# Two blocks of a seven-product dense layer by turns, with finer weight jobs and another order of operands, in a fused FNet, Mish and gate kernel

## The chip, the cores and the metric

The kernel runs on one core of a Trainium2 chip. The metric is the device time of one execution in microseconds (us); lower is better. Times are from executions on the chip; one further execution was recorded by the hardware profiler.

## What is computed

The input x is 2048 x 640, in float32. Two branches are mixed by a gate:

```
g = sigmoid((x * gate_w).sum(-1))                 # one value per row
a = C_re @ (x @ Wd_re.T) - C_im @ (x @ Wd_im.T)   # 2048 x 2048 and 640 x 640 DFT matrices
h = x @ w1 + b1;  b = mish(h) @ w2                # 640 -> 1728 -> 640, mish(v) = v * tanh(softplus(v))
out = g * a + (1 - g) * b
```

The change lies in the first dense product, x @ w1, with its bias and Mish.

## The kernel before

**Arithmetic.** TensorE (PE) multiplies blocks of 128 x 128 by 128 x 512. For float32 accuracy each operand is split in a high and a low part (`split`, L82: a copy on ScalarE, ACT, L80, and a subtraction on VectorE, DVE, L77), and one product takes three matmuls (`mm3`, L91). The large products are done in the Strassen-Winograd way: seven products of half-size blocks in place of eight, at the price of sums of the operands beforehand and sums of the results behind.

**Order of work.** The whole program is a list of steps, each with matmuls for PE, the preparation of its operands (splits, sums, and the loads that these need), and work behind it (`post`, `at`). The loop at L967 writes the instructions out in that order: at step i it first runs the preparations of all steps up to i + 7 (i + 6 in the dense stage, `LEAD_D`), issuing loads of up to nine steps further ahead (`AHEAD`) while more than three buffers are free; then the matmuls of step i, stores that are due, the work behind the step, and then, as long as its own clock says that DVE is more than 1 us behind PE and `wait_until` allows it, parts of jobs that have no fixed place (L1006). Each engine runs its instructions in the order in which they were written out, and each waits for its own operands. All loads and stores go through SP's queue (loads L978, stores L987), in order too.

**Jobs.** A job is a generator that stops at each `yield`. `job_go` (L151) sets `wait_until = i + yielded value`: with 0 the next part may follow in the same step, with 1 in the next step at the earliest. `w1_job` (L552) splits the weights of one block and makes their sums, in four parts. Behind the w1 jobs follow y products (`gate_y`), and then the weights of the output stage ("top", w2c, w2r and "low" jobs). `need` runs a job's remaining parts at once where a step's preparation wants them. No job parts are started in steps from four before to twelve after the start of the dense stage (`quiet`).

**Buffers.** There are 20 of 128 x 512 in float32 (f), 10 pairs for split operands (rh, rl; some more are lent from the weights' buffers), 26 pairs for split weights (wh, wl), 4 for raw weights (fx), and 8 PSUM banks (ps). Each kind is a list from which the longest free one is taken. A buffer that was stored can be taken again as soon as its store has been written out; the load or copy into it waits until the store has landed. A result is stored three steps after it was made. A job that loads f buffers is only taken up if its own and eight more are free.

**The dense stage** has 104 steps, counted here from 0. Steps 0 to 7 compute the columns of h that the blocks leave over (`dense_rest`). The other columns are six blocks fp = 0 to 5, each of the column chunks fa = fp and fb = fp + 6. `dense_first` does them for the first half of the rows (tp = 0, steps 8 to 55), and then for the second half (tp = 1, steps 56 to 103); the output stage follows at 104. A block takes one turn of eight steps:

| step of the turn | operand | bank | matmuls | work behind it |
|---|---|---|---|---|
| 0 p1 | a11 | a (new) | 6 | ACT copies a into an f buffer ("snap") |
| 1 p5 | s1 | b (new) | 6 | snap of b |
| 2 | d2 | d (new) | 3 | none |
| 3 p6 | s2 | a goes on | 6 | snap of a, called u2 |
| 4 p3 | s4, d1 | b goes on | 9 | DVE adds u2 to b; Mish; b is free |
| 5 p7 | s3 | a goes on | 6 | DVE adds a to the snap of b |
| 6 p2 | a12, d1 | c (new) | 9 | DVE adds c and d to the snaps; c, d free; Mish one and two steps later |
| 7 p4 | a22, d2 | a goes on | 9 | Mish of a two steps later, then a is free |

The operands (x and its sums s1 to s4) are split once for each half and kept in rh/rl buffers through its six turns; `free` gives them back in the turn of the last block. `sums_of` (L687) loads four blocks of x and makes the four sums, for k = 0 and 1. At which step each is prepared is written out by hand in the lists at L939 and L941; a preparation listed for step n runs six steps earlier.

Of the kernel before, what the change touches and what calls it, by code (L numbers as in the profile page):

```python
# [10 lines left out]
OP = mybir.AluOpType  # L11

S, D, F = 2048, 640, 1728
P = 128
# [7 lines left out]
FP = 6  # L22
# [23 lines left out]
def fnet_mish_gate(ctx: ExitStack, tc: tile.TileContext, xn, xt, c_re, c_im, wd_re, wd_im,  # L46
# [28 lines left out]
    def tt(o, a, b, op):  # L75
        clock["dve"] += 0.14 + 0.54 * a.shape[-1] / N
        nc.vector.tensor_tensor(o, a, b, op=op)  # L77

    def copy(o, a, scale=1.0):
        nc.scalar.activation(o, a, AF.Copy, scale=scale)  # L80
# [10 lines left out]
    def mm3(ps, ah, al, bh, bl, start, stop):  # L91
        mm(ps, ah, bh, start, False)
        mm(ps, ah, bl, False, False)
        mm(ps, al, bh, False, stop)

    def part(w, a, b):
        return w[0][:, a:b], w[1][:, a:b]
# [454 lines left out]
    def w1_job(f, ga, gb):  # L552
        t = FS.get()
        a, b, c = W.get(), W.get(), W.get()
        if f % KD == 0:
            T2B[f // KD] = W.get()
        split(*a, ga)
        split(*part(b, 2 * P, 5 * P), gb[:, 2 * P:])
        yield 0

        tt(ga[:, A2], gb[:, A2], ga[:, A2], OP.subtract)
        tt(gb[:, A2], gb[:, B2], gb[:, A2], OP.subtract)
        tt(t[:, A2], gb[:, B2], ga[:, A2], OP.subtract)
        tt(t[:, B2], ga[:, B2], t[:, A2], OP.subtract)
        yield 0
        split(*part(b, 0, 2 * P), t[:, B2])
        split(*part(c, 0, 2 * P), ga[:, A2])
        yield 0
        split(*part(c, 2 * P, 4 * P), gb[:, A2])
        split(*part(c, 4 * P, 5 * P), t[:, :P])  # L570
        split(*part(T2B[f // KD], f % KD * P, f % KD * P + P), t[:, P:2 * P])
        FS.put(t)
        FX.put(ga, gb)
        W1[f] = (a, b, c)
# [106 lines left out]
    def dense_first(tp, end, ops):  # L681


        t1, t2 = 2 * tp, 2 * tp + 1
        n0 = len(steps)

        def sums_of(k):  # L687
            raw = [(("xs", tp, a, k), xt[t, kk])
                   for a, t, kk in ((21, t2, k), (22, t2, k + 2), (11, t1, k), (12, t1, k + 2))]

            def prep():
                a21, a22, a11, a12 = (RAW.pop(r[0]) for r in raw)
                s1 = FS.get()
                tt(s1, a21, a22, OP.add)
                tt(a21, a11, a21, OP.subtract)
                tt(a22, s1, a11, OP.subtract)
                tt(a12, a12, a22, OP.subtract)
                FS.put(a11)
                XS[k] = {"s1": s1, "s2": a22, "s3": a21, "s4": a12}
            return raw, prep  # L700

        def make(name):
            def prep():
                if name[0] == "s":
                    for k in range(2):
                        x_split((name, k, tp), XS[k].pop(name))
                elif name[0] == "d":
                    x_split((name, 0, tp), RAW.pop(("xd", tp, name)))
                else:
                    for k in range(2):  # L710
                        x_split((name, k, tp), RAW.pop(("xo", tp, name, k)))
            return prep

        def sub(fp, ops, then=()):

            def mms():
                a, b, c = W1[fp]
                for bank, name, blk, start, stop in ops:
                    if start:
                        H[bank] = psum.get()  # L720
                    for k in range(2):
                        mm3(H[bank], *blk(a, b, c, k), *X[name, k, tp], start and k == 0, stop and k == 1)
                for bank, name, w, start, stop in then:
                    if start:
                        H[bank] = psum.get()
                    mm3(H[bank], *part((a, b)[w], 4 * P, 5 * P), *X[name, 0, tp], start, stop)
            return mms

        def at_cols(which, c0):
            return lambda a, b, c, k: part((a, b, c)[which], c0 + k * P, c0 + k * P + P)  # L730

        def t2_at(fp):
            return lambda a, b, c, k: part(c, 4 * P, 5 * P) if k == 0 else \
                part(T2B[fp // KD], fp % KD * P, fp % KD * P + P)

        def snap(name, bank):
            f = KEEP[name] = FS.get()
            copy(f, H[bank])

        def pop(bank):  # L740
            psum.put(H.pop(bank))

        def add(bank, f):
            tt(f, H[bank], f, OP.add)
            return f

        def out_act(f, t, o, src):
            mish(o, src, f)
            store(asc[f][t], o, o)

        for fp in range(FP):
            fa, fb = fp, fp + FP
            over = fp == FP - 1

            def free(*names, over=over):
                if over:
                    x_free(*[(n, k, tp) for n in names for k in range(2 if n[0] != "d" else 1)])

            def p1_post(free=free):
                snap("p1", "a")  # L760
                free("a11")

            def p5_post(free=free):
                snap("p5", "b")
                free("s1")

            def p6_post(free=free):
                snap("u2", "a")
                free("s2")

            def p3_post(free=free, fb=fb):
                o = add("b", KEEP.pop("u2"))
                pop("b")
                out_act(fb, t1, o, o)
                free("s4")

            def p7_post(free=free):
                add("a", KEEP["p5"])
                free("s3")

            def p2_post(free=free, fa=fa, fb=fb):
                c11, c22 = add("c", KEEP.pop("p1")), add("d", KEEP.pop("p5"))
                pop("c")
                pop("d")
                i = clock["step"]
                at(i + 1, lambda: out_act(fa, t1, c11, c11))
                at(i + 2, lambda: out_act(fb, t2, c22, c22))
                free("a12", "d1")

            def p4_post(free=free, fa=fa, fp=fp):  # L790
                ps = H.pop("a")

                def last():
                    out_act(fa, t2, FS.get(), ps)
                    psum.put(ps)
                at(clock["step"] + 2, last)
                free("a22", "d2")
                if end:
                    W.put(*W1[fp])
                    if fp in (KD - 1, FP - 1):  # L800
                        W.put(T2B[fp // KD])

            step([], [lambda fp=fp: need(("w1", fp))], sub(fp, [("a", "a11", at_cols(0, 0), True, True)]), p1_post)
            step([], [], sub(fp, [("b", "s1", at_cols(2, 0), True, True)]), p5_post)
            step([], [], sub(fp, [], [("d", "d2", 1, True, True)]))
            step([], [], sub(fp, [("a", "s2", t2_at(fp), False, True)]), p6_post)
            step([], [], sub(fp, [("b", "s4", at_cols(1, 2 * P), False, False)], [("b", "d1", 1, False, True)]), p3_post)
            step([], [], sub(fp, [("a", "s3", at_cols(2, 2 * P), False, True)]), p7_post)
            step([], [], sub(fp, [("c", "a12", at_cols(0, 2 * P), True, False)], [("c", "d1", 0, False, True)]), p2_post)
            step([], [], sub(fp, [("a", "a22", at_cols(1, 0), False, False)], [("a", "d2", 0, False, True)]), p4_post)  # L810
        for name, i in ops:
            if name[0] == "k":
                raw, prep = sums_of(int(name[1:]))
                steps[i][0].extend(raw)
                attach.append((i, prep))
                continue
            kk = {"a11": (t1, 0), "a12": (t1, 2), "a22": (t2, 2), "d1": (t1, 4), "d2": (t2, 4)}.get(name)
            if name[0] == "d":
                steps[i][0].append((("xd", tp, name), xt[kk]))
            elif kk:  # L820
                steps[i][0].extend((("xo", tp, name, k), xt[kk[0], kk[1] + k]) for k in range(2))
            attach.append((i, make(name)))
# [107 lines left out]
    for tp in range(2):  # L930
# [7 lines left out]
    n0 = nd + 8  # L938
    dense_first(0, False, [("k0", n0 + 2), ("k1", n0 + 2), ("s1", n0 + 3), ("s2", n0 + 4), ("s4", n0 + 6), ("s3", n0 + 7)])  # L939
    n0 = len(steps)  # L940
    dense_first(1, True, [("a11", n0 - 1), ("k0", n0), ("k1", n0 + 1), ("s1", n0 + 1), ("d2", n0 + 2), ("s2", n0 + 3),  # L941
                          ("s4", n0 + 4), ("d1", n0 + 4), ("s3", n0 + 5), ("a12", n0 + 6), ("a22", n0 + 7)])
    narrow.update(range(nd, len(steps)))
    quiet = range(nd - 4, nd + 13)
    n_dense = len(steps)
# [114 lines left out]
```

## Time and profile before

| | |
|---|---|
| median of 3 runs | 891.66 us (891.64 to 891.80) |
| the profiled execution, its time | 893.29 us |
| its span | 891.4 us |
| PE's mean granted clock | 0.996 of full |
| moved to and from memory | 215.22 MB, mean 241 GB/s |

The profile names instructions by engine, line and tiles (f<-ps is a write of an f buffer from a PSUM bank). Since splits, sums and copies go through helpers, their line is the helper's: L77 is any DVE operation on two tensors, L80 any ACT copy, L89 any matmul, L618 Mish. The view of waits lists for each engine what it waited for, with the sum, the number of times and the longest. In the timeline a row is start, duration, engine, line, operation and tiles, and in square brackets the idle time before it and what ended it. Matmuls overlap: each is recorded with 0.39 us, and the next starts some 0.23 us after it. A table by stretches gives the busy time of each engine in windows counted from the start of the span.

### The profile page before, as it was taken

The page shows a single profiled execution, that of the slowest core. Times are in us where ns is not written, and L with a number is a line of the kernel's source. Part 1 is how long each engine was busy: PE and PEld are TensorE (multiplying, and loading weights), DVE is VectorE, ACT ScalarE, POOL GpSimd, SP SyncE. Part 2 cuts the span into 40 slices and gives each one's busy share as a digit, 9 for nine tenths or more (in the row PEclk, how much of TensorE's full clock was granted, in tenths as well). Part 3 has the DMA queues.
Part 4 walks back from the last instruction along what each step waited for, and adds up shares of the span by engine and source line. Part 5 has one row for each costly group of instructions (what it writes and reads, how often), then busy time and mean ns, then how long its engine had stood idle before and what let it go on. Part 6 is the DMA issues. An engine that isn't in the chain of part 4 may idle for free.

```text
span 891.4 us, 12188 instructions
## 1 busy us (share of the span) xinstructions
PE 864.6 (97%) x3780; PEld 711.3 (80%) x3780; DVE 714.5 (80%) x1243; ACT 479.3 (54%) x910; POOL 0.2 (0%) x4
## 2 busy tenths in 40 slices
PE   8999999999999999999999999898899999999995
PEld 6888888888888888888888888687688788888884
DVE  5899997899799668998997987764844897689986
ACT  5665645454565545647665576544555665442630
POOL 0000000000000000000000000000000000000000
PEclk9999999999999999999999999999999999999998
DMA  9865669597979564768868793589575667467753
GB/s 321 309 214 186 238 209 308 154 318 235 319 268 335 207 217 160 262 226 268 282 213 290 263 316 135 181 309 358 194 260 176 240 226 246 144 229 238 268 208 129
DMA packets 118064, 215.22 MB, mean 241 GB/s; under 512 B 13424, under 2 KB 15600, under 8 KB 118000
## 3 DMA queue, kind: packets, MB, share of 16 engines
q1 hardware_dynamic: 118000, 214.46, 70.3%
q8 instruction: 29, 0.48, 0.2%
q14 instruction: 35, 0.29, 0.1%
HBM read 168.80 MB, written 45.61 MB: 241 GB/s over the span
## 4 chain that ended last, share of the span: by engine, by line
PE 91%; DVE 4%; DMA 2%; issue 1%; ACT 1%; SPq 0%; DVEq 0%; ACTq 0%
PE ps L89 91%; DVE f L77 2%; DMA act<-f 1%; DVE wl L77 1%; DVE fx L77 1%; DMA f<-in_xn_dram 1%; ACT wh L80 0%; DVE rl L77 0%; SPq L978 0%; ACT rh L80 0%; ACT f L618 0%; ACT f L80 0%; DMA f<-in_xt_dram 0%; SPq L958 0%; SPq L987 0%
## 5 line engine op out<-in xcount | busy, mean ns | idle before, releaser
L89 PE MATMUL ps<-rh,wh 128*128 128x512 f32 x1067 | 416.6, 391 | 8.1 <-ACT f L80 3.9
L89 PE MATMUL ps<-rh,wl 128*128 128x512 f32 x1053 | 410.2, 390 | 0.0
L89 PE MATMUL ps<-rl,wh 128*128 128x512 f32 x1052 | 409.8, 390 | 0.0
L80 ACT ACTIVATE rh<-f 128x512 fp32r<-128x512 f32 x412 | 243.6, 624 | 150.8 <-DVE f L77 104.1
L77 DVE TENSOR_TENSOR rl<-f,rh 128x512 fp32r<-128x512 f32 x410 | 266.7, 685 | 51.3 <-ACT rh L80 50.7
L89 PEld LDWEIGHTS ps<-rh,wh 128*128 128x128 f32 x1067 | 200.8, 188 | 52.7 <-ACT f L80 5.6
L89 PEld LDWEIGHTS ps<-rh,wl 128*128 128x128 f32 x1053 | 198.2, 188 | 41.1
L89 PEld LDWEIGHTS ps<-rl,wh 128*128 128x128 f32 x1052 | 198.2, 188 | 41.2
L77 DVE TENSOR_TENSOR f<-f,f 128x512 f32<-128x512 f32 x311 | 212.9, 689 | 15.0 <-DMA u<-f 5.4
L80 ACT ACTIVATE f<-ps 128x512 f32<-128x512 f32 (+1 forms) x147 | 86.5, 595 | 104.5 <-PE ps L89 82.8
L77 DVE TENSOR_TENSOR f<-ps,f 128x512 f32<-128x512 f32 x87 | 57.4, 686 | 56.5 <-PE ps L89 56.5
L80 ACT ACTIVATE wh<-f 128x512 fp32r<-128x512 f32 (+2 forms) x160 | 70.1, 477 | 50.7 <-DVE f L77 41.3
L77 DVE TENSOR_TENSOR wl<-f,wh 128x512 fp32r<-128x512 f32 (+2 forms) x159 | 75.5, 505 | 19.2 <-ACT wh L80 19.0
L89 PE MATMUL ps<-wh,wh 128*128 128x512 f32 x201 | 78.8, 392 | 6.5 <-DVE f L77 4.2
L89 PE MATMUL ps<-wl,wh 128*128 128x512 f32 x196 | 76.3, 389 | 0.0
L89 PE MATMUL ps<-wh,wl 128*128 128x512 f32 x195 | 75.9, 389 | 0.0
L77 DVE TENSOR_TENSOR wl<-fx,wh 128x640 fp32r<-128x640 f32 (+3 forms) x80 | 42.3, 551 | 16.9 <-ACT wh L80 16.9
L618 ACT ACTIVATE f<-f,b1s 128x512 f32<-128x512 f32 x36 | 25.9, 720 | 51.9 <-DVE f L77 51.9
L89 PEld LDWEIGHTS ps<-wh,wh 128*128 128x128 f32 x201 | 37.7, 188 | 16.5 <-DVE f L77 5.0
L80 ACT ACTIVATE wh<-fx 128x128 fp32r<-128x128 f32 (+5 forms) x81 | 39.2, 511 | 6.8 <-DMA fx<-in_xn_dram 2.7
L89 PEld LDWEIGHTS ps<-wl,wh 128*128 128x128 f32 x196 | 36.8, 188 | 7.4
L89 PEld LDWEIGHTS ps<-wh,wl 128*128 128x128 f32 x195 | 36.6, 188 | 7.6
(40 smaller groups left out, 162.4 us busy)
## 6 DMA issues: line engine op xcount, KB each, us to landing
f<-in_c_re_dram SPq DMA_DIRECT2D x128, 256.0 KB, 4.1
f<-in_c_im_dram SPq DMA_DIRECT2D x128, 256.0 KB, 4.0
f<-act SPq DMA_DIRECT2D x82, 256.0 KB, 5.2
f<-u SPq DMA_DIRECT2D x80, 256.0 KB, 4.5
f<-in_xt_dram SPq DMA_DIRECT2D x64, 256.0 KB, 4.4
act<-f SPq DMA_DIRECT2D x52, 256.0 KB, 4.8
u<-f SPq DMA_DIRECT2D x40, 256.0 KB, 3.2
y<-f SPq DMA_DIRECT2D x40, 256.0 KB, 4.1
```

Of the source, the lines that this page charges most:

```text
L77: nc.vector.tensor_tensor(o, a, b, op=op)
L80: nc.scalar.activation(o, a, AF.Copy, scale=scale)
L89: nc.tensor.matmul(ps, a, b, start=start, stop=stop, skip_group_check=True)
L618: nc.scalar.activation(o[rows], src[rows], AF.Mish, bias=b1s[rows, f:f + 1])
```

## The change

Three things are changed, and the computation stays the same.

Two blocks (0 and 1, then 2 and 3, then 4 and 5) are done by turns: step 0 of the first, step 0 of the second, step 1 of the first, and so on, 16 steps for two. Banks and kept results are therefore named by block as well. The three `yield 0` of `w1_job` become `yield 1`. And the operands of the second half are prepared at other steps; n0 is the second half's first step (56).

```diff
@@ w1_job
         split(*a, ga)
         split(*part(b, 2 * P, 5 * P), gb[:, 2 * P:])
-        yield 0
+        yield 1
...
-        yield 0
+        yield 1
         split(*part(b, 0, 2 * P), t[:, B2])
         split(*part(c, 0, 2 * P), ga[:, A2])
-        yield 0
+        yield 1
@@ dense_first
-                        H[bank] = psum.get()
+                        H[bank, fp] = psum.get()
...
-        def snap(name, bank):
-            f = KEEP[name] = FS.get()
-            copy(f, H[bank])
+        def snap(name, bank, fp):
+            f = KEEP[name, fp] = FS.get()
+            copy(f, H[bank, fp])
...
-        for fp in range(FP):
-            fa, fb = fp, fp + FP
-            over = fp == FP - 1
+        def parts(fp):
+
+            fa, fb, over = fp, fp + FP, fp == FP - 1
...
-            step([], [lambda fp=fp: need(("w1", fp))], sub(fp, [("a", "a11", at_cols(0, 0), True, True)]), p1_post)
-            step([], [], sub(fp, [("b", "s1", at_cols(2, 0), True, True)]), p5_post)
...
+            return [
+                ([lambda: need(("w1", fp))], sub(fp, [("a", "a11", at_cols(0, 0), True, True)]), p1_post),
+                ([], sub(fp, [("b", "s1", at_cols(2, 0), True, True)]), p5_post),
...
+        for fp in range(0, FP, 2):
+            for two in zip(parts(fp), parts(fp + 1)):
+                for p in two:
+                    step([], *p)
@@ the second half's list
-    dense_first(1, True, [("a11", n0 - 1), ("k0", n0), ("k1", n0 + 1), ("s1", n0 + 1), ("d2", n0 + 2), ("s2", n0 + 3),
-                          ("s4", n0 + 4), ("d1", n0 + 4), ("s3", n0 + 5), ("a12", n0 + 6), ("a22", n0 + 7)])
+    dense_first(1, True, [("a11", n0 - 8), ("k0", n0 - 4), ("k1", n0 - 3), ("s1", n0 - 2), ("d2", n0), ("s2", n0 + 2),
+                          ("s4", n0 + 4), ("d1", n0 + 5), ("s3", n0 + 7), ("a12", n0 + 9), ("a22", n0 + 11)])
```

The order of the eight steps of a block, their matmuls and the work behind them stay as they were, and so does the first half's list.

More of the change, by code (lines that the diff above doesn't have):

```diff
@@ L719, in mms @@
                     if start:
-                        H[bank] = psum.get()
+                        H[bank, fp] = psum.get()
                     for k in range(2):
-                        mm3(H[bank], *blk(a, b, c, k), *X[name, k, tp], start and k == 0, stop and k == 1)
+                        mm3(H[bank, fp], *blk(a, b, c, k), *X[name, k, tp], start and k == 0, stop and k == 1)
                 for bank, name, w, start, stop in then:
                     if start:
-                        H[bank] = psum.get()
-                    mm3(H[bank], *part((a, b)[w], 4 * P, 5 * P), *X[name, 0, tp], start, stop)
+                        H[bank, fp] = psum.get()
+                    mm3(H[bank, fp], *part((a, b)[w], 4 * P, 5 * P), *X[name, 0, tp], start, stop)
             return mms
@@ L734, in t2_at, with pop, add @@
                 part(T2B[fp // KD], fp % KD * P, fp % KD * P + P)
-        def snap(name, bank):
-            f = KEEP[name] = FS.get()
-            copy(f, H[bank])
[L740 to L744, printed above, removed]
+        def snap(name, bank, fp):
+            f = KEEP[name, fp] = FS.get()
+            copy(f, H[bank, fp])
+        def pop(bank, fp):
+            psum.put(H.pop((bank, fp)))
+        def add(bank, name, fp, keep=False):
+            f = KEEP[name, fp] if keep else KEEP.pop((name, fp))
+            tt(f, H[bank, fp], f, OP.add)
             return f
@@ L749, in out_act, with free, p1_post, p5_post @@
             store(asc[f][t], o, o)
-        for fp in range(FP):
-            fa, fb = fp, fp + FP
-            over = fp == FP - 1
-            def free(*names, over=over):
+        def parts(fp):
+            fa, fb, over = fp, fp + FP, fp == FP - 1
+            def free(*names):
                 if over:
                     x_free(*[(n, k, tp) for n in names for k in range(2 if n[0] != "d" else 1)])
-            def p1_post(free=free):
-                snap("p1", "a")
+            def p1_post():
+                snap("p1", "a", fp)
                 free("a11")
-            def p5_post(free=free):
-                snap("p5", "b")
+            def p5_post():
+                snap("p5", "b", fp)
                 free("s1")
-            def p6_post(free=free):
-                snap("u2", "a")
+            def p6_post():
+                snap("u2", "a", fp)
                 free("s2")
-            def p3_post(free=free, fb=fb):
-                o = add("b", KEEP.pop("u2"))
-                pop("b")
+            def p3_post():
+                o = add("b", "u2", fp)
+                pop("b", fp)
                 out_act(fb, t1, o, o)
                 free("s4")
-            def p7_post(free=free):
-                add("a", KEEP["p5"])
+            def p7_post():
+                add("a", "p5", fp, True)
                 free("s3")
[L781 to L784, printed above, removed]
+            def p2_post():
+                c11, c22 = add("c", "p1", fp), add("d", "p5", fp)
+                pop("c", fp)
+                pop("d", fp)
                 i = clock["step"]
@@ L788, in p2_post, with p4_post @@
                 free("a12", "d1")
-            def p4_post(free=free, fa=fa, fp=fp):
-                ps = H.pop("a")
+            def p4_post():
+                ps = H.pop(("a", fp))
                 def last():
@@ L801, in p4_post @@
                         W.put(T2B[fp // KD])
-            step([], [lambda fp=fp: need(("w1", fp))], sub(fp, [("a", "a11", at_cols(0, 0), True, True)]), p1_post)
-            step([], [], sub(fp, [("b", "s1", at_cols(2, 0), True, True)]), p5_post)
[L805 to L810, printed above, removed]
+            return [
+                ([lambda: need(("w1", fp))], sub(fp, [("a", "a11", at_cols(0, 0), True, True)]), p1_post),
+                ([], sub(fp, [("b", "s1", at_cols(2, 0), True, True)]), p5_post),
+                ([], sub(fp, [], [("d", "d2", 1, True, True)]), None),
+                ([], sub(fp, [("a", "s2", t2_at(fp), False, True)]), p6_post),
+                ([], sub(fp, [("b", "s4", at_cols(1, 2 * P), False, False)], [("b", "d1", 1, False, True)]), p3_post),
+                ([], sub(fp, [("a", "s3", at_cols(2, 2 * P), False, True)]), p7_post),
+                ([], sub(fp, [("c", "a12", at_cols(0, 2 * P), True, False)], [("c", "d1", 0, False, True)]), p2_post),
+                ([], sub(fp, [("a", "a22", at_cols(1, 0), False, False)], [("a", "d2", 0, False, True)]), p4_post)]
+        for fp in range(0, FP, 2):
+            for two in zip(parts(fp), parts(fp + 1)):
+                for p in two:
+                    step([], *p)
         for name, i in ops:
```

## The prediction

> **What bounds the kernel now.** I read the page first (span, busy time), then the list of waits of PE, then PE's own timeline around those waits, then the busy table by stretches, then what ACT, DVE and SP did in the worst stretch.
>
> ```profile
> span 891.4 us, 12188 instructions
> ...
> PE 864.6 (97%) x3780; PEld 711.3 (80%) x3780; DVE 714.5 (80%) x1243; ACT 479.3 (54%) x910; POOL 0.2 (0%) x4
> ```
>
> PE is the bound: 3780 matmuls, and the change keeps their number. So the only time that it can win is time in which PE stands still. The waits of PE over the whole run say how much of that is caused by the other engines' results:
>
> ```profile
> PE ps L89 <- ACT f L80: 6.2, 6, 1.6
> PE ps L89 <- DVE f L77: 5.7, 3, 2.8
> ```
>
> Nine waits, 11.9 us. PE's timeline shows that all nine lie between 566 and 709 us, in three groups, and all in the dense product (first column the start, in square brackets the idle time and what ended it):
>
> ```profile
> 565.84 0.39 PE L89 MATMUL ps<-rh,wh 128*128 128x512 f32 x1
> ...
> 566.29 0.39 PE L89 MATMUL ps<-rh,wl 128*128 128x512 f32 x1
> 568.30 0.50 PE L89 MATMUL ps<-rh,wh 128*128 128x512 f32 x1 [1.62 <-ACT f L80]
> ...
> 571.11 0.50 PE L89 MATMUL ps<-wh,wh 128*128 128x512 f32 x1 [0.46 <-ACT f L80]
> ...
> 576.19 0.50 PE L89 MATMUL ps<-wh,wh 128*128 128x512 f32 x1 [1.39 <-DVE f L77]
> ...
> 619.64 0.50 PE L89 MATMUL ps<-rh,wh 128*128 128x512 f32 x1 [0.90 <-ACT f L80]
> ...
> 622.68 0.50 PE L89 MATMUL ps<-rh,wh 128*128 128x512 f32 x1 [1.37 <-ACT f L80]
> ...
> 626.50 0.50 PE L89 MATMUL ps<-wh,wh 128*128 128x512 f32 x1 [1.46 <-ACT f L80]
> ...
> 633.02 0.50 PE L89 MATMUL ps<-wh,wh 128*128 128x512 f32 x1 [2.81 <-DVE f L77]
> 633.36 0.40 PE L89 MATMUL ps<-wl,wh 128*128 128x512 f32 x1
> ...
> 703.74 0.50 PE L89 MATMUL ps<-wh,wh 128*128 128x512 f32 x1 [0.37 <-ACT f L80]
> ...
> 708.90 0.50 PE L89 MATMUL ps<-rh,wh 128*128 128x512 f32 x1 [1.47 <-DVE f L77]
> ```
>
> Undisturbed matmuls start 0.225 us apart (565.84 to 566.29 holds two; the planner's own constant, L29, is 0.2267, used below). A wait costs more than its idle time: the matmul of 566.29 would have been followed at 566.52, and was at 568.30, 1.78 late for 1.62 idle; and the one after a wait comes 0.34 later (633.02 to 633.36), 0.11 over the cadence. So each costs 0.27 more: 11.9 + 9 x 0.27 = 14.3 us. By groups: first (3.47 + 0.8) 4.3, second (6.54 + 1.1) 7.6, third (1.84 + 0.5) 2.4.
>
> The table by stretches (PE, PEld, DVE, ACT, POOL busy, then PE's granted clock, DMA share, GB/s) shows what surrounds them:
>
> ```profile
> 549.50:565.00 15.50, 15.50 (x70) 12.71 (x68) 9.72 (x20) 9.29 (x20) 0.00 (x0) 1.00 0.25 76
> 565.00:577.00 12.00, 8.53 (x36) 6.08 (x35) 9.17 (x24) 6.65 (x17) 0.00 (x0) 1.00 0.60 199
> 577.00:596.00 19.00, 19.00 (x85) 15.58 (x84) 12.87 (x25) 10.14 (x20) 0.00 (x0) 1.00 0.82 290
> 596.00:617.00 21.00, 21.00 (x95) 17.38 (x94) 9.54 (x15) 6.14 (x10) 0.00 (x0) 1.00 1.02 378
> 617.00:634.00 17.00, 10.46 (x42) 7.37 (x41) 11.81 (x19) 9.88 (x18) 0.00 (x0) 1.00 0.71 245
> 660.00:696.00 36.00, 36.00 (x161) 29.80 (x160) 14.68 (x30) 17.21 (x33) 0.00 (x0) 1.00 0.67 222
> 696.00:711.00 15.00, 13.16 (x57) 10.21 (x56) 13.13 (x28) 11.23 (x24) 0.00 (x0) 1.00 0.57 205
> 711.00:735.00 24.00, 24.00 (x108) 19.86 (x107) 22.33 (x46) 15.80 (x34) 0.00 (x0) 1.00 0.64 216
> ```
>
> Even in the disturbed stretches neither DVE nor ACT is full (9.17 and 6.65 of 12; 11.81 and 9.88 of 17). PE waits for the delay of one result, not for throughput.
>
> **What the waits are.** In one turn of eight steps (6, 6, 3, 6, 9, 6, 9, 9 matmuls, 54 in all, 12.2 us) a bank is four times added to again after ACT or DVE has read it: a after p1 and after u2, b after p5, a after p7. Between the reading step and the next use lie 9 matmuls each time: 9 x 0.2267 = 2.04 us. The copy itself takes 0.59 us, the add 0.69:
>
> ```profile
> L77 DVE TENSOR_TENSOR f<-ps,f 128x512 f32<-128x512 f32 x48 | 32.0, 687 | 40.4 <-PE ps L89 40.4
> ...
> L77 DVE TENSOR_TENSOR f<-f,f 128x512 f32<-128x512 f32 x28 | 18.2, 686 | 0.2
> ...
> L77 DVE TENSOR_TENSOR rl<-f,rh 128x512 fp32r<-128x512 f32 x16 | 10.6, 686 | 9.2 <-ACT rh L80 9.2
> ...
> L80 ACT ACTIVATE f<-ps 128x512 f32<-128x512 f32 x36 | 21.3, 592 | 17.4 <-PE ps L89 11.8 <-DMA y<-f 4.2 <-DMA act<-f 0.8
> ```
>
> so some 1.4 us of foreign work ahead of it on its in-order engine is enough to stop PE. First and third group: splits of weights stand ahead of it. Second group: the operands of the second half, and a transfer:
>
> ```profile
> 611.11 2.87 SPq L978 DMA_DIRECT2D f<-in_xt_dram  x3
> 614.08 0.85 SPq L987 DMA_DIRECT2D y<-f  x2
> ...
> 618.99 0.60 ACT L80 ACTIVATE f<-ps 128x512 f32<-128x512 f32 x1 [4.20 <-DMA y<-f]
> ...
> 620.75 0.69 DVE L77 TENSOR_TENSOR rl<-f,rh 128x512 fp32r<-128x512 f32 x1 [6.12 <-ACT rh L80]
> ```
>
> The copy at 618.99 goes into an f buffer whose y store had not landed; that store was issued at 614.08 or just after, having stood on SP's queue behind three loads that took 2.87 us. One transfer takes about 5 us to land between 596 and 640, the DMA engines being full (share 1.02) from 596 to 617:
>
> ```profile
> f<-in_xt_dram SPq DMA_DIRECT2D x16, 256.0 KB, 5.3
> act<-f SPq DMA_DIRECT2D x11, 256.0 KB, 4.9
> y<-f SPq DMA_DIRECT2D x9, 256.0 KB, 5.1
> ```
>
> **The change, part by part.** Steps are counted from the first dense step as 0: the first half is 8 to 55, the second 56 to 103.
>
> Two blocks by turns. The double turn takes 16 steps, 108 matmuls. The four distances become 24 matmuls at least (p1 to s2: 6+6+6+3+3; p5 to s4: 6+3+3+6+6; u2 to s3: 6+9+9; p7 to a22: 6+9+9), 5.44 us in place of 2.04. No instruction is added. Banks: six are held at most until s4 gives b back, and c takes the one longest free; the last banks of the previous double turn are given back in the first two steps of the next, so no step waits for a bank. If the wider distance were all, what a group loses now plus 2.04 is the lag that it needs, and what exceeds 5.44 stays: first 4.3 + 2.04 = 6.3, 0.9 left; second 9.6, 4.2 left; third 4.4, none. 5.1 us would stay.
>
> Weight work in finer parts. A w1 job has four parts on DVE of 1.36, 1.64, 0.82 and 0.96 us (planner's prices, L76, whose 0.68 for 512 columns agrees with the 686 ns above). Three of them could be queued in one step, and now one is. Counting the planner's rule forward by hand, the parts left for blocks 2 to 5 fall on steps 13 to 26, against 13 to 25 now: the same DVE work over as long a time, but without three parts at step 13. Block 3 is wanted sooner: its first step moves from 32 to 25, so it must be split by step 19, and my count ends it at 18; were it late, one part of at most 1.64 us would be forced in, still below 5.44. Laying these parts, copies and adds on ACT and DVE one after another, the latest copy of the next double turn lands 1.2 us before PE wants it. Bounds: the 0.9 us above, and nothing. I take nothing.
>
> Other order of the second half's operands. 16 splits and 8 sums, each 0.686 on DVE, run at steps 49 to 57 now: with the four adds of a turn 24 x 0.686 + 4 x 0.687 = 19.2 us of DVE work beside 60 matmuls, 13.6 us. That is the burst of the second group (the y products before it are what fills the DMA engines). After, they run at steps 42 to 61: 126 matmuls, 28.6 us, for 24 x 0.686 + 8 x 0.687 = 22.0 us, 77%. From split to first use there are 9 to 14 steps in place of 6 or 7. Each moved step takes its loads along: they pass ahead of y stores and loads on SP's queue, starting 7 steps sooner (33 for 40). The rh/rl buffers suffice: the first half's operands come free from step 41 on in pairs, always ahead of the split that takes them.
>
> f buffers (20). Copies and results on their way to a store hold 27 buffer-steps in a turn of 8 (3.4 on average), and 78 in a double turn of 16 (4.9). The operands wait in 16 buffers at their peak now, in 11 after. With the y products throttled by their own rule (10 free; what is put off finds room at 660 to 696, DVE busy 14.68 of 36) my count gives 2 or 3 free in steps 38 to 43 and 4 or more after, against 5 or fewer over some ten steps (42 to 52) now. So one or two copies may still wait for a store. Bounds for that: none, and the 4.2 us that the wider distance alone would leave. I take one stall of the kind at 619.64, 0.90 + 0.27 = 1.2 us, the smallest row of the group, since a wait like that of 4.20 plus the copy's 0.59 is within 5.44.
>
> W buffers. Block f's weights come free in the second half with step 8f + 7 of it now; those of blocks 0, 2 and 4 come free seven steps later after. The last two groups of low jobs that ran at steps 95 to 103 must wait for step 102. That takes splits off the third group's stretch, which is one more reason for it to go, and moves about 8.2 us of DVE work (two jobs of 4.1 by L76) past 711 us, where DVE is busy 22.33 of 24 already. There every operand is split seven steps of 9 matmuls ahead, 14.3 us, and the jobs' own deadlines (steps 110 and 118 for the first three) are kept by my count, the last job ending near step 119 in place of 114. I cost it at nothing: bounds 0 and 8.2 - 1.67 = 6.5 us, DVE's idle time in that row taken off.
>
> Sum. The profiled execution took 893.29 for its span of 891.4; the median of the three runs is 891.66, 1.63 less, and the stalls are as long in both as far as one profile can say. 891.66 - 14.3 + 1.2 = **878.5 us**; the floor is 877.3 (some smaller slow matmuls could give a few tenths more).
>
> [...] Full use of the clock is part of the sum. PE's granted clock is 1.00 in every row of the table, the one with the 2.81 us gap included, with blocks that go through the eight banks by turns already. What a lost clock would cost is seen at the start:
>
> ```profile
> 12.12 0.63 PE L89 MATMUL ps<-rh,wh 128*128 128x512 f32 x1
> 12.55 0.63 PE L89 MATMUL ps<-rl,wh 128*128 128x512 f32 x1
> ```
>
> 0.43 us apart, 0.20 over the cadence: a single double turn of 108 matmuls at that rate costs 21.6 us, and ends at 877.3 + 21.6 = 898.9. [...] No row here bears it out, so that case gets 0.02.
>
> **The rivals.** (1) Only the wider distance counts: the spread preparation is eaten by f buffers waiting for stores. For: the 4.20 and 6.12 us rows come from a transfer, not from work. Against: fewer loads at once. 891.66 - 14.3 + 5.1 = 882.5. Chance 0.19. (2) The delayed low jobs make DVE late in the out stage: 877.3 + 6.5 = 883.8 at most. For: 22.33 of 24. Against: the lead of seven steps. Chance 0.07. (3) The change doesn't do what it says: the delay is a chain of ACT and DVE waiting for each other (gaps with both below 80% busy) that grows with any allowance; 891.66 within 0.2%. Chance 0.04. (4) Slower: f buffers run short through two whole double turns, not for some six steps. The shortage now costs 7.6 us in the ten steps or so in which it acts; over 32 steps at that rate 24 us, in place of 7.6, less the 6.7 of the other groups: 891.66 + 16.4 - 6.7 = 901.4. It decides where fewer than four buffers are free throughout: a double turn with operands takes a buffer about every 1.25 us, and four of those make a transfer's 5 us. For: 4.9 held in place of 3.4. Against: 11 operands waiting in place of 16. Chance 0.06.
>
> **How the numbers follow.** A measurement of this kernel can tell about 0.2%, 1.8 us. Forecast 0.62 with its own range of 876.7 to 881.5 (none of the 1.2 left and 0.6 of slow matmuls gained; or 4.2 left, 877.3 + 4.2). Rivals 1 and 2 end faster too: faster 0.62 + 0.19 + 0.07 = 0.88; same 0.04; slower 0.06 + 0.02 = 0.08. The range of 876.5 to 884.0 takes in the forecast and rivals 1 and 2, and leaves 0.12 out.
>
> **What would show it.** Right: no wait of PE on ACT or DVE between 560 and 580 or 690 and 710, at most one or two of about 1 us near 600 to 620; DVE's burst after 620 gone; the end of the last matmul 13 us sooner. Rival 1: ACT's copies still waiting for y or act stores by 4 us, with PE waits of 1 to 3 us there. Rival 2: new PE waits between 700 and 740. Rival 4: such waits from 590 to 640. The clock: a granted clock under 1.00 in the dense stretch. Wrong altogether would be a first group still there, since there no transfer is involved.

## The result and the profile after

The changed kernel takes **877.04 us** (median of 4, 876.85 to 878.54) where before takes 891.65 (median of 4, 889.34 to 891.80). The ratio is 0.9839, 95% interval 0.982 to 0.9857. (Among the experiments below, e3 had one execution of four that took 1091.14 us at a granted clock of 0.754; its median there is that of the other three.)

The page of the changed kernel, span and busy times:

```profile
span 875.3 us, 12178 instructions
...
PE 860.4 (98%) x3780; PEld 711.6 (81%) x3780; DVE 713.4 (82%) x1243; ACT 478.1 (55%) x910; POOL 0.2 (0%) x4
```

The same work in a span 16.1 us shorter. All that PE (its matmuls) waits for in the whole run is now this (waited for, sum, times, longest), and both rows belong to the start of the program:

```profile
PE ps L89 <- ACT rh L80: 2.7, 1, 2.7
PE ps L89 <- DVE rh L881: 1.6, 1, 1.6
```

The stretches of the three groups (PE, PEld, DVE, ACT, POOL busy, granted clock, DMA share, GB/s) show PE full in all of them:

```profile
565.00:577.00 12.00, 12.00 (x55) 9.94 (x54) 10.78 (x25) 8.17 (x20) 0.00 (x0) 1.00 0.86 293
...
617.00:634.00 17.00, 17.00 (x77) 14.08 (x75) 9.40 (x17) 11.66 (x21) 0.00 (x0) 1.00 0.67 233
696.00:711.00 15.00, 15.00 (x68) 12.43 (x67) 13.51 (x30) 11.79 (x26) 0.00 (x0) 1.00 0.63 212
```

ACT still waits for stores to land, as the prediction allowed. ACT's timeline of the changed kernel in the first half's last turn:

```profile
600.98 0.60 ACT L80 ACTIVATE f<-ps 128x512 f32<-128x512 f32 x1 [1.19 <-DMA y<-f]
...
608.68 0.60 ACT L80 ACTIVATE f<-ps 128x512 f32<-128x512 f32 x1 [2.62 <-DMA act<-f]
```

PE's rows around the second one:

```profile
606.35 0.39 PE L89 MATMUL ps<-rh,wl 128*128 128x512 f32 x1
...
612.01 0.39 PE L89 MATMUL ps<-wh,wh 128*128 128x512 f32 x1
```

The copy at 608.68 reads block 5's bank a, into which step p6 puts its last matmul at 606.35; PE adds to that bank again at 612.01 (p7). The copy ends at 609.28, 2.7 us ahead. With nine matmuls between, PE would have wanted the bank at 608.6, and by this sum would have stood.

**Where the time came from.** I call time lost in a step the distance from its first matmul to the next step's first, less 0.2267 for each matmul. Before, the dense stage loses 4.5, 7.8 and 2.5 us in its three groups, 14.7 in all; the changed kernel loses nothing. That is the whole gain: 891.65 - 14.7 = 876.9. The two profiles differ by 1.4 us more, and that lies in the first 14 us, see the end.

### The profile page after: what moved, and what is told of

It is laid out like the page before. It is cut to its first block, busy times and chain, and to the rows that moved or that the text cites. A ratio compares the mean times of both kernels' runs of the same rounds, so it can differ in the third digit from the quotient of the medians.

```text
span 875.3 us, 12178 instructions
## 1 busy us (share of the span) xinstructions
PE 860.4 (98%) x3780; PEld 711.6 (81%) x3780; DVE 713.4 (82%) x1243; ACT 478.1 (55%) x910; POOL 0.2 (0%) x4
## 4 chain that ended last, share of the span: by engine, by line
PE 97%; DVE 1%; DMA 1%; issue 0%; SPq 0%; ACT 0%
PE ps L89 97%; DVE f L77 1%; DMA f<-in_xn_dram 1%; DVE fx L77 0%; SPq L966 0%; ACT wh L80 0%; ACT rh L80 0%; SPq L986 0%
## 5 line engine op out<-in xcount | busy, mean ns | idle before, releaser
L77 DVE TENSOR_TENSOR wl<-f,wh 128x512 fp32r<-128x512 f32 (+2 forms) x156 | 73.0, 501 | 20.4 <-ACT wh L80 20.4
L77 DVE TENSOR_TENSOR wl<-fx,wh 128x640 fp32r<-128x640 f32 (+3 forms) x83 | 44.5, 556 | 17.3 <-ACT wh L80 17.3
L80 ACT ACTIVATE wh<-fx 128x128 fp32r<-128x128 f32 (+5 forms) x84 | 41.0, 514 | 9.0 <-DMA fx<-in_xn_dram 3.5
```

## The experiments

They ran on four chips, on which the kernel before takes 892.4 to 893.7 us; ratios are to before on the same chip. The last columns are the time lost near 570, 620 and 700 us, from one profile of each run.

| | median us | ratio (interval) | first | second | third |
|---|---|---|---|---|---|
| before (its own profile) | 891.65 | 1 | 4.5 | 7.8 | 2.5 |
| changed | 877.04 | 0.984 (0.982 to 0.986) | 0 | 0 | 0 |
| e1 turns alone | 881.81 | 0.989 (0.986 to 0.992) | 0 | 4.4 | 0 |
| e2 turns, yield | 881.18 | 0.987 (0.984 to 0.990) | 0 | 4.3 | 0 |
| e3 turns, list | 877.88 | 0.984 (0.981 to 0.987) | 0 | 0 | 0 |
| e4 yield alone | 889.24 | 0.996 (0.995 to 0.998) | 1.7 | 8.0 | 2.4 |
| e8 before, y late | 898.91 (one run) | none | 4.4 | 7.2 | 0.4 |
| e9 before, no sums | 889.12 | 0.996 (0.993 to 0.998) | 4.4 | 4.4 | 2.4 |
| e11 before, sums early | 887.54 | 0.994 (0.992 to 0.995) | 4.5 | 2.9 | 2.5 |
| e12 before, low late | 890.14 | 0.997 (0.996 to 0.998) | 4.5 | 7.9 | 0.4 |

In the second column e1, e4, e8 and e12 hold some 1.5 us each in which PE ran at half clock behind a wait (the mean granted clock of these profiles is 0.993, 0.993, 0.988 and 0.993, that of before 0.996). Without that e4 and e12, which change nothing near 620 us, lose about 6.5 there where before lost 7.8, so a figure of one profile in this column is good to about 1 us.

**e1 to e4: the three edits taken apart.** My theory A was the prediction's own arithmetic: the wider distance takes 3.4 us off each group, and what exceeds it stays. e1 is the changed kernel with the old `yield 0` and the old list; e2 has the old list only; e3 the old yields only; e4 is the kernel before with the new yields:

```diff
e1, e2:
-    dense_first(1, True, [("a11", n0 - 8), ("k0", n0 - 4), ("k1", n0 - 3), ("s1", n0 - 2), ("d2", n0), ...
+    dense_first(1, True, [("a11", n0 - 1), ("k0", n0), ("k1", n0 + 1), ("s1", n0 + 1), ("d2", n0 + 2), ...
e1, e3 (w1_job, three times):
-        yield 1
+        yield 0
e4 (w1_job of before, three times):
-        yield 0
+        yield 1
```

e1: 

> Two blocks by turns, with the weight job's three `yield 0` and the old list of the second half. Theory A (the prediction's rival 1: the distance of 5.44 us takes 3.4 us off the delay of each group, the lists and yields do the rest): 5.1 us of PE waits stay, 0.9 near 570 and 4.2 near 620, so 877.0 + 5.1 = 882.1 us. Theory B (the distance alone is enough): no PE wait in the dense stage, 877.0 us. Theory C (the second group is DVE's burst and shifts with any allowance): 7.6 us stay near 620, 884.6 us.

e2: 

> The changed kernel with the old list of the second half. Theory A: 4.2 us of PE waits stay near 620, none near 570 and 700, 881.2 us. Theory B: 877.0 us with no wait. Theory C: 884.6 us.

e3: 

> The changed kernel with the weight job's three `yield 0`. Theory A: at most 0.9 us of PE waits stay near 570, none near 620, 877.0 to 877.9 us. Theory B: 877.0 us. A theory in which the finer parts are what ends the first group: its 4.3 us stay, 881.3 us.

e4: 

> The kernel before with `yield 1` in the weight job, blocks one after the other. Theories A and B (the first group comes from the distance of 2.04 us): within 1.5 us of before, 890.2 to 891.7 us, with the waits near 570 still there. A theory in which three parts in one step set off the first group: its 4.3 us go, 887.4 us.

Measured: 881.81, 881.18, 877.88 and 889.24. e1, e2 and e3 are where theory A put them, and theory B (distance is enough) falls with e1 and e2. But the parts of the 5.1 us are others. In e1 nothing is left of the first group, where I had 0.9. In the second, PE waits once for 2.1 us; PE's timeline of e1 there:

```profile
617.54 0.51 PE L89 MATMUL ps<-wh,wh 128*128 128x512 f32 x1
...
619.52 0.39 PE L89 MATMUL ps<-rh,wl 128*128 128x512 f32 x1
622.00 0.80 PE L89 MATMUL ps<-wh,wh 128*128 128x512 f32 x1 [2.09 <-DVE f L77]
622.59 0.63 PE L89 MATMUL ps<-wl,wh 128*128 128x512 f32 x1
623.02 0.63 PE L89 MATMUL ps<-wh,wl 128*128 128x512 f32 x1
...
625.15 0.47 PE L89 MATMUL ps<-rl,wh 128*128 128x512 f32 x1
625.46 0.39 PE L89 MATMUL ps<-rh,wl 128*128 128x512 f32 x1
625.68 0.39 PE L89 MATMUL ps<-rh,wh 128*128 128x512 f32 x1
```

The wait is 2.09, and behind it the matmuls start 0.43 us apart until 625.15: PE's clock had gone to half (granted clock 0.50 in that stretch). Of the 4.4 us some 1.5 are that. So the 4.2 that I had forecast for waits was some 2.9, and the sum was right partly by luck.

e4 is a miss for theory A. It expected the first group to stay whole; 1.7 us of 4.5 are left, and the view of waits has one wait of PE there:

```profile
572.52 0.50 PE L89 MATMUL ps<-wh,wh 128*128 128x512 f32 x1 [0.76 <-DVE f L77]
```

So the distance ends the first group without the finer parts (e1, e3: 0). The finer parts take 2.8 of its 4.5 us by themselves (the ratio 0.9962 is 3.4 us, of which the dense stage shows 2.5; the rest is inside its interval), and once there is the distance they add nothing (e3 against the changed kernel: 0 and 0).

**e8, e9, e11: what makes the second group.** The profile of before shows both a copy that waits 4.20 us for a store and a burst of splits and sums. Its longest piece is the eight sums, which DVE does in one row:

```profile
621.96 5.40 DVE L77 TENSOR_TENSOR f<-f,f 128x512 f32<-128x512 f32 x8
```

e8 takes the y products' transfers away from the kernel before; e9 leaves the second half's sums out (its result is another); e11 makes the sums, and their loads, five steps earlier.

```diff
e8 (the y products' jobs, now behind the "top" weights):
     stage_jobs(fin, [("top", k) for k in range(FP)])
+    for t in range(TG):
+        for d in range(KD):
+            jobs.append(Job(("yg", t, d), ...
e9 (sums_of):
+                if tp:
+                    s1 = a11
+                else:
...
e11:
-    ("k0", n0), ("k1", n0 + 1),
+    ("k0", n0 - 5), ("k1", n0 - 4),
```

e8: 

> The kernel before with the y products queued behind the output stage's top weights, so that their loads and stores leave the stretch before 617 us; DVE's burst of splits and sums stays. If the second group is made by transfers (f buffers whose store has not landed, SP's queue): the group near 617 to 634 us shrinks from 7.6 to 3 us or less. If it is DVE's burst: 5 us or more of waits stay there. The end of the run is moved too (y products run into the output stage), so only the waits near 610 to 635 us are to be read, not the time.

e9: 

> The kernel before without the eight sums of x for the second half (the unsummed blocks are used in their place, so the second half's products are others): 8 x 0.686 = 5.5 us less DVE work in the burst, with the same loads and splits. If the burst makes the second group: its 7.6 us fall to about 2 to 3, 886 us. If transfers make it: 5 us or more stay, 889 us or more.

e11: 

> The kernel before with the second half's sums five steps earlier (the splits can't be moved: one block after the other gives no rh/rl buffer back before step 48). If DVE's burst makes the second group: 5.5 us of DVE work leave it, and 2 to 3 us of 7.6 stay. If transfers make it: the loads now meet the y products' transfers earlier, and 5 us or more stay, wherever they fall.

In e8 no wait of ACT for a transfer is left; its waits between 605 and 636 us are:

```profile
ACT f L618 <- DVE f L77: 8.9, 4, 2.8
ACT f L80 <- PE ps L89: 3.2, 2, 2.0
ACT rh L80 <- DVE f L77: 2.4, 2, 2.0
ACT f L80 <- ACT f L618: 0.9, 1, 0.9
```

and yet the group loses 7.2 us of 7.8 (1.5 of them in a stretch of half clock behind its longest wait; PE's waits are 5.0 us in place of 6.5). Leave out the sums instead, and it shrinks to 4.4. In e9 a copy still waits for a y store, and the two waits of PE behind it (1.59 and 0.47) are most of what stays:

```profile
619.88 0.60 ACT L80 ACTIVATE f<-ps 128x512 f32<-128x512 f32 x1 [4.89 <-DMA y<-f]
```

e11 loses 2.9, but it doesn't separate the two: with the loads moved, no copy waits for a store behind 610 us either. So the burst makes most of the group by itself; the transfer wait lies beside it, and is what comes next once the burst is smaller. The time of e8 isn't to be read: its delayed y products cost 8.7 us at one step of the output stage.

**e5 to e7: how much delay the distance takes.** An added loop in `snap` of either kernel makes the copy 4 or 8 times more, for p1 alone:

```diff
     copy(f, H[bank, fp])
+    for _ in range(4 if name == "p1" else 0):
+        copy(f, H[bank, fp])
```

e5: 

> The kernel before, with each of the 12 copies of p1 made five times in a row (same source, same target), so that bank a's reader ends about 4 x 0.5 = 2.0 us later. Distance theory: 2.04 us between p1 and the next use of bank a, less 0.8 for the copy itself, leaves 1.2, so each of the 12 places loses some 0.8 to 1.1 us, 10 to 13 us in all: about 903 us. Throughput theory (ACT is 54% busy, so 24 us more of its work lies beside PE): within 1 us of before.

e6: 

> The changed kernel with the same 4 more copies at each p1. Distance theory: 5.44 - 0.8 - 2.0 leaves 2.6 us, no or nearly no PE wait, 877 to 878.5 us. If the change's gain were from the lighter ACT and DVE stretches alone and not from the distance, the same 10 to 13 us would be lost as in the kernel before: 887 to 890 us.

e7: 

> The changed kernel with 8 more copies at each p1: 4.0 us. Distance theory: 5.44 - 0.8 - 4.0 leaves 0.6 us, less than the delay that ACT has in its busy stretches, so the waits come back, at bank a after p1: 2 to 12 us, 879 to 889 us.

Measured: e5 915.93 us, ratio 1.027 (1.024 to 1.030); e6 887.63, ratio 0.993 (0.991 to 0.996); e7 927.61, ratio 1.040 (1.037 to 1.043). The throughput theory falls with e5. But all three cost more than I expected, and e6 and e7 are clear misses. First, the copies are dearer than 0.5 us: ACT's rows in e5 and e7,

```profile
597.27 3.12 ACT L80 ACTIVATE f<-ps 128x512 f32<-128x512 f32 x5 [1.98 <-PE ps L89]
```

```profile
615.20 5.65 ACT L80 ACTIVATE f<-ps 128x512 f32<-128x512 f32 x9 [3.37 <-PE ps L89]
620.75 0.68 ACT L618 ACTIVATE f<-ps,b1s 128x512 f32<-128x512 f32 x1
621.32 5.63 ACT L80 ACTIVATE f<-ps 128x512 f32<-128x512 f32 x9
```

0.63 each into the same buffer, so 4 more are 2.5 us, and 8 are 5.0. In e5 that takes what is left of 2.04 in all twelve places: 38.2 - 14.7 = 23.5 us, 2.0 each on average, three stretches of half clock included (mean granted clock 0.991, before 0.996); five places with nothing else near lose 1.5. Second, and this is the flaw in my reading of 5.44 us: in e7 the second block's copies (621.32) start only when the first block's nine and a Mish are through. The 24 matmuls between a copy and the next use hold the other block's copy too, on the same engine. What counts is the work of both blocks, here 5.65 + 0.57 + 5.63 = 11.9 us, against the 30 matmuls (6.8 us) from the first block's p1 to the second block's s2. The excess, 5.1 us, is about what each of the six places loses at that step (4.7 to 5.8). (The dense stage of e7 loses 50.4 us; the larger part of the other 20 is half clock behind these waits: the mean granted clock is 0.977, the changed kernel's 0.996.) In e6 the same sum is near 6.8, so by it nothing would be lost, and yet 10.7 us are, in six places, from 0.4 to 4.0. Other work on ACT comes on top of the sum: in the worst place splits of weights run until 578.63,

```profile
577.49 1.14 ACT L80 ACTIVATE wh<-fx 128x640 fp32r<-128x640 f32 x2
578.54 3.10 ACT L80 ACTIVATE f<-ps 128x512 f32<-128x512 f32 x5
```

and a stretch of half clock follows (mean granted clock of e6 0.994). The 10.7 are less than half of e5's 23.5. Distance bought by turns is real, but it is shared.

**e10: fewer f buffers.** `NFS` 20 becomes 18 in the changed kernel.

> The changed kernel with 18 f buffers in place of 20. By the prediction's rival 4 (f buffers short through two double turns, fewer than four free): free ones are at 2 to 4 in steps 38 to 51 in place of 38 to 44, so copies wait for stores of 4 to 5 us again and PE waits come back near 600 to 620 us: 880 to 885 us. If the distance covers such waits for good: 877 us and no wait.

Measured 883.55, ratio 0.990 (0.988 to 0.992). The time is in the range of the first reading, and for another reason: the dense stage loses nothing, though by the code one to four buffers are free at the start of steps 39 to 51. The run loses 6.2 us in earlier stages, the largest part at 193 us (2.6) and 239 us (1.6). ACT's copies did wait for stores there (3.77 us at 540.56, 1.91 at 611.77), and PE didn't, so such waits are covered even then, and the prediction's rival 4 falls. (By the code 14 of the 20 y products then come at step 64 or later, in place of 9, and their transfers with them.)

**e12: the third group.** The low jobs of before, all but the first, are held until dense step 102, as they are in the changed kernel:

```diff
+            elif loaded and loaded[0][0].key == ("out", "low", 1) and i < nd + 102:
+                break
             elif loaded and loaded[0][2] + (5 if i in narrow else 3) <= i and ...
```

> The kernel before with the output stage's low jobs 1 to 5 held back until dense step 102, as the later freed weight buffers hold them back in the changed kernel (from there they run at nearly the same steps in both). If the third group is made by these jobs' splits standing ahead of the copies and adds: its 2.4 us go, 890.2 us where before is 892.6. If it would need the wider distance: it stays. In both cases the prediction's price of nothing for the delayed jobs wants no new wait behind 711 us; at its other bound, 6.5 us, the kernel would be slower than before by 4 us.

Measured 890.14, ratio 0.997 (0.996 to 0.998). The third group falls from 2.5 to 0.4 us, and no wait comes behind 711 us, where DVE is as full as I feared. The table by stretches of e12:

```profile
696.00:711.00 15.00, 14.92 (x66) 12.06 (x65) 9.98 (x19) 9.34 (x19) 0.00 (x0) 1.00 0.39 134
711.00:735.00 24.00, 24.00 (x108) 19.88 (x107) 22.84 (x48) 18.25 (x39) 0.00 (x0) 1.00 0.68 228
```

So the later return of weight buffers, which I had looked at as a cost, nearly ends the third group by itself. In e8 the low jobs run from step 110 on, and the group is at 0.4 there too (0.7 more are lost at 665 us). Whether the distance alone would do it isn't shown: e1 to e3 have both.

## Why the prediction was right

- **The size of what could be won** was right: 14.3 us counted from nine waits and 0.27 for each; 14.7 by steps.
- **What stays** was 1.2 us and measured 0. The one term taken too large is the copy waiting for a store: such waits came (1.19 and 2.62 us) and stayed below the distance, with 2.7 us to spare.
- **The first group.** That 0.9 us of it would stay if the distance were all was wrong: nothing stayed (e1). That sum took a group's three waits as the lag of one result; whether this is why isn't shown. And I had priced the finer parts at nothing only as an addition to the distance; alone they are worth 2.8 us (e4).
- **The second group** was right in that the distance leaves part of it and the list takes that part (e1, e2: 4.4 and 4.3; e3: 0). My prediction named a burst and a transfer side by side, and rival 1 leaned on the transfer; e8 and e9 give the larger share to the burst.
- **The third group** is gone, and the delayed low jobs alone take 2.1 of its 2.5 us (e12). The prediction had them as one more reason beside the distance, which wasn't tried without them.
- **The delayed low jobs** cost nothing, as taken (rival 2 falls: no wait of PE behind 711 us in the changed kernel, with DVE busy 22.64 of 24 there, nor in e12, with 22.84; by the code the last of them ends at step 116, not 119).
- **5.44 us for each block** was wrong as a measure of the reserve: it is shared with the other block (e6, e7). It didn't show, since one copy of 0.59 us for each block is far below it.
- **The clock** stayed at 1.00 in the dense stage of the changed kernel. No run of it shows the double turn at half clock, 21.6 us, that the prediction gave 0.02: with the banks of two blocks in turn no matmul of that stage ran at half clock, and the four runs take 876.85 to 878.54 us. (The 0.43 us between matmuls behind that sum stands beside a granted clock of 1.00 in the profile of before, 10.00 to 13.40 us; e1 shows 0.43 at 0.50.) Half clock came in e1, e4 to e8 and e12, behind waits, with a mean granted clock of 0.977 to 0.994 in these profiles.

Not tried: the new list without turns. It can't be had, because one block after the other gives no rh/rl buffer back before step 48. And finer parts, earlier sums and held low jobs together without turns, which by the columns above would leave some 5 us (1.7 + 2.9 + 0.4, an estimate), more than the changed kernel's none.

## What to carry to other kernels

Where the busiest engine waits for results of engines that are not full, count the work between the result's producer and its next use, and what can stand ahead of it on its in-order engine: either the distance is widened or the foreign work is moved; here the first group needed only the distance, and the third lost most of its 2.5 us by moved work. Interleaving two independent blocks widens the distance without new work, but the other block's own work lies in it as well. And a group of waits may have two causes, and more than half of it may stay with either gone: take them away one at a time before naming one.

## What the runs showed of the hardware

**A wait of 2 to 3 us had half clock behind it in some runs, and not in others.** In e1 PE waited 2.09 us and then ran at half rate for 3.2 us (above). The stretch in the table (PE busy first, then PEld, DVE, ACT, POOL, granted clock, DMA share, GB/s):

```profile
621.89:625.31 3.42, 3.31 (x8) 2.64 (x9) 3.42 (x7) 2.13 (x4) 0.00 (x0) 0.50 0.90 267
```

In e4 it waited 2.38 us, up to 623.62, and the matmuls from 624.33 to 627.31 start 0.43 apart; in e8 2.78 us, with the matmuls behind it 0.43 apart until 632.14:

```profile
629.04 0.74 PE L89 MATMUL ps<-wh,wh 128*128 128x512 f32 x1 [2.78 <-DVE f L77]
629.58 0.63 PE L89 MATMUL ps<-wl,wh 128*128 128x512 f32 x1
630.01 0.63 PE L89 MATMUL ps<-wh,wl 128*128 128x512 f32 x1
...
632.56 0.40 PE L89 MATMUL ps<-rh,wl 128*128 128x512 f32 x1
```

Before, the wait of 2.81 us up to 633.02 had no such tail: the next matmuls start at 633.36, 633.59 and 633.82, and the granted clock is 1.00 from 617 to 634 us and from 634 to 660. Nor had e2's of 2.12 us up to 623.31, with the next at 623.64, 623.88 and 624.11. So the length of a wait alone did not decide it; what did isn't shown.

**The start moved the total by over a microsecond.** In the profile of before the first matmuls run at half rate (0.43 us apart) until 13.40 us, in that of the changed kernel until about 11.1, with full rate from here on:

```profile
11.57 0.39 PE L89 MATMUL ps<-rh,wh 128*128 128x512 f32 x1
11.80 0.39 PE L89 MATMUL ps<-rl,wh 128*128 128x512 f32 x1
```

The same code, and 1.4 us between the two where the first dense step starts (526.80 and 525.43). That is the rest of the 16.1 us of the spans, and it may be one reason why single executions of a kernel differ by 1 to 2 us.
